# Memsets and small copies of an attention + feed-forward kernel on VectorE instead of GpSimd, with every engine's order made anew

## The chip, the cores and the metric

The kernel runs on one core of one Trainium2 chip. The metric is the device time of one execution in microseconds (us). A core has five engines that run side by side, each through its own list of instructions in order: TensorE (PE; its weight loads are listed as PEld), VectorE (DVE), ScalarE (ACT), GpSimd (POOL) and SyncE (SP), which only issues transfers (DMAs) here. GpSimd and SyncE each issue DMAs. An engine that meets an instruction whose inputs are not there waits, and all behind it in its list waits too.

## The reference

Attention with a decay ("forgetting attention"), then a bilinear feed-forward layer on its result. 8 batches x 8 heads, 576 positions, head size 64; the feed-forward layer takes 4608 tokens of 512 to 1536 and back.

```python
scores = scale * np.matmul(q, k.transpose(0, 1, 3, 2))
log_f = np.log(np.clip(f, 0.0001, 1.0))
cum = np.cumsum(log_f, axis=-1)
decay = cum[:, :, :, None] - cum[:, :, None, :]
scores = np.where(causal, -1000000000.0, scores + decay)
attn = softmax(scores)                       # max, exp, sum, divide
attn_out = np.matmul(attn, v)
x = attn_out.transpose(0, 2, 1, 3).reshape(B * S, H * D)
out = (x @ w_a) * (x @ w_b) @ w_out
```

## The kernel before

**Work.** Everything is written as a list of operations (class `Op`, L142): each has an engine (or a choice of two), a planned duration, and dependencies. The operations' own functions issue the instructions. Which operation comes when is not decided by the program: `ORDER` (L1069) is a long table of operation numbers, and `CHOICE` (L1177) gives the engine of those that have a choice. `laid_out` (L1181) reads both, and the instructions are issued in that order, so that each engine's list is the order of its operations in the table. Waits between engines are put in where data or buffers require it.

**Attention.** Heads go in pairs t = 0 to 31 (four pairs per batch). For a pair, the 576 queries are five blocks (the last of 64). `qk_group` (L443) makes the scores of a group of blocks in a PSUM tile `sc` (a ring of two buffers); groups are blocks (1, 0), (2), (3), (4). For batch 0 (`DECP`) the decay enters by matmuls of `crow` (the cumulated logarithms, high and low parts) with a one-hot column of `pick`; the causal mask by matmuls of `low` with `neg64`. Then VectorE reduces the maximum (L546), ScalarE takes the exponential with its sum (L603, PA or PB), VectorE takes the reciprocal of the sum (L613), GpSimd normalises (L621), and P is transposed, for the first pairs by TensorE (`psP`, L641), and multiplied with v (L663, L679). From batch 1 on, VectorE adds the decay from the tile `spread` in one instruction with the maximum (L572).

**Feed-forward.** As soon as four pairs of a batch have delivered 256 tokens or more, TensorE can do `psa`, `psb` (L950) and `pso` (L970) for them. These fill TensorE between the groups of scores.

**The head of the program.** k and q of batch 0 and 1 are loaded by GpSimd's queue with a cast (`load_qk`, L274, DMAs at L286), transposed on TensorE (`pe_transpose`, L299, tiles `psT` in a PSUM ring `ff` of three buffers, two buffers for each call) and copied to kT and qT by ScalarE or VectorE (`pe_evict`, L313). f is loaded by SP (L180), clipped on VectorE (L192), its logarithm taken on ScalarE (L226), cumulated on VectorE (`scan`, L195), and copied to `crow` as a high part (L230) and a low part (L200, on VectorE or GpSimd). ScalarE loads the table of the logarithm first (L220) and that of the exponential later (`o_e`, L239), each 1.28 us in the trace. `f_ones` (L182) sets three tiles with ones on VectorE. Weights are loaded by GpSimd's queue (`weights`, L412, DMAs at L424).

**What the change touches.** `identity` (L72) makes the 128x128 identity `ident16` on GpSimd, which the transposes and the one-hot columns need. `constants` (L81, GpSimd) sets `pickh`, `neg64` and `low`, copies 32x32 pieces of the identity to `pick` and `pickh`, and cuts `neg64` and `low` to their masks with six `affine_select`. `paddings` (L100, GpSimd) zeroes `qd`, `lowd`, parts of `PB` and of `nv`, and copies `low` to `lowd`. `wake` (L75) issues dummy matmuls on the identity, in 24 operations of two each (a wake pair), which keep TensorE busy while nothing else can run; they write the one PSUM buffer `pv`, so each pair waits for the pair before it.

Of the kernel before, what the change touches and what calls it, by code (L numbers as in the profile page):

```python
# [25 lines left out]
def kernel(  # L26
# [11 lines left out]
    nc = tc.nc  # L38
# [4 lines left out]
    NSB = (S + 127) // 128  # L43
# [16 lines left out]
    neg64 = perm.tile([128, 64], FP16, tag="neg64", name="neg64")  # L60
# [20 lines left out]
    def constants():  # L81
        for x in pickh:
            nc.gpsimd.memset(x, 0.0)
        for m in range(4):
            x = slice(32 * m, 32 * m + 32)
            nc.gpsimd.tensor_copy(out=pick[x, :], in_=ident16[x, x])
            nc.gpsimd.tensor_copy(out=pickh[m // 2][x, :], in_=ident16[x, x])
        nc.gpsimd.memset(neg64, 0.0)
        for x in low:
            nc.gpsimd.memset(x, 1.0)  # L90
        for h in range(2):
            nc.gpsimd.affine_select(out=neg64[HP[h], :], in_=neg64[HP[h], :],
                                    compare_op=mybir.AluOpType.not_equal, fill=NEGBIG, base=0,
                                    pattern=[[-1, 64]], channel_multiplier=1)
            for half in range(2):
                x = low[half][HP[h], :]
                nc.gpsimd.affine_select(out=x, in_=x, compare_op=mybir.AluOpType.is_gt, fill=0.0,
                                        base=64 * half, pattern=[[-1, 128]], channel_multiplier=1)

    def paddings():  # L100
        for x in (*qd, lowd):
            nc.gpsimd.memset(x, 0.0)
        for r in HP:
            nc.gpsimd.tensor_copy(out=lowd[r, r], in_=low[0][r, 0:64])
        for x in PB:
            nc.gpsimd.memset(x[:, 12, 64:128], 0.0)
        for i in range(2):
            nc.gpsimd.memset(nv[i][64:128, NSB - 1, :, :], 0.0)
# [104 lines left out]
    o_c = Op("POOL", 3.3, lambda _: constants(), [o_i], prio=-300, name="const")  # L213
# [28 lines left out]
    o_p = Op("POOL", 4.0, lambda _: paddings(), [o_c], prio=-100)  # L242
# [823 lines left out]
    for n in cuts:  # L1066
# [3 lines left out]
        65 1 0 45 2 49 53 57 67 3 69 28-30 36 31-35 4-8 46 9 47 37 38 10 50 48 51 52 43 11 78 12 123 54 13 39 81  # L1070
# [4 lines left out]
        162 385 386 260 163 221 261 80 199 22 244 23 387 24 200 99 245 105 207 263 208 100-102 388 106 252 253  # L1075
# [7 lines left out]
        403 306 351 396 352 398 354 345 308 353 397 307 405 277 494 1783 406 322 166 1784-1786 167 1788 356 1787  # L1083
        355 1789 407 408 1790 248 1792 1791 357 409 249 1793 410 287 1794 1795 309 1796 323 1798 310 1797 316
        311-313 358 250 1799 317 324 251 318 1800 495 339 211 1801 496 497 404 506 436 425 437 361 212 319 426
# [10 lines left out]
        480 1866 563 1868 1867 582 600 692 697 481 553 554 1864 1870 1871 1869 586 1872 1873 587 1874-1876 1878  # L1096
        562 603 1880 555 556 693 698 601 511 559 1877 1879 588 591 1881 589 1882 1884 1883 576 1885 1886 593
        1887 1888 611 590 583 592 569 578 570 610 584 585 1890 1891 594 1889 1892 604 1893 605 606 595 612 618
        596 571 577 613 699 1894 484 607 700 701 485 619 614 615 625 597 1895 694-696 646 704 709 1865 718 626
        486 609 1896-1898 1900 1902 620 1899 621 1903 1901 1904 1906 1908 608 628 1907 627 598 599 1860 716 632  # L1100
        487 622 1905 633 647 656 710 617 602 728 623 1909 705 634 1910-1912 637 638 629 635 1913 639-641 636
# [8 lines left out]
        754 762 763 904 772 792 1975 798 811 766 801 813 915 1977-1979 905 803 908 820 866 821 823 799 906 802  # L1110
# [114 lines left out]
```

## Time and profile before

| | us |
|---|---|
| median of 3 runs | 409.13 (408.86 to 409.19) |
| the profiled execution | 408.86 |
| its span, first to last instruction | 407.1 |
| TensorE busy | 396.3 |
| VectorE busy | 301.6 |
| ScalarE busy | 282.5 |
| GpSimd busy | 262.3 |

A row of the order of time reads: start, duration (us), engine, line, operation, output<-inputs, shapes, count, and in brackets the idle time of the engine before it with what ended that wait. A row with a count above one merges neighbours of one kind, from the start of the first to the end of the last. In the table of stretches, each engine's column is its busy time in that stretch, with the number of its instructions in parentheses.

### The profile page before, as it was taken

To read this page: it belongs to the slowest core of one execution; us is meant where nothing else is said; L and a number is where in the kernel's file an instruction comes from. 1 tells how busy PE (TensorE), PEld (TensorE's weight loads), DVE (VectorE), ACT (ScalarE), POOL (GpSimd) and SP (SyncE) were. 2 spreads that over 40 slices of the span, in tenths; PEclk is the share of its full clock that TensorE was granted. 3 is DMA by queue.
4 is the path that set the end of the run, shared out by engine and by line. 5 is a ranking of instruction groups with operands and counts; after the bars stand their busy time and mean duration, and the time that the engine had idled before them with its cause. 6 is when DMAs were issued, how large, how long until landed. Compare 5 with 4: busy or idle time off the path is not lost.

```text
span 407.1 us, 11321 instructions
## 1 busy us (share of the span) xinstructions
PE 396.3 (97%) x4028; PEld 213.4 (52%) x4028; DVE 301.6 (74%) x1007; ACT 282.5 (69%) x796; POOL 262.3 (64%) x490
## 2 busy tenths in 40 slices
PE   6899999999999999999999999999999999999996
PEld 2457675766755554444445454444444444444552
DVE  3887998997979778878868789688888874442241
ACT  3898988888977778778787877568785873231230
POOL 8997697778876786886787767849666555000000
PEclk9999999999999999999999999999999999999999
DMA  8999998999999999999999999999895768100102
GB/s 126 205 190 199 152 217 194 203 271 233 249 196 221 320 229 208 276 199 229 204 275 253 278 237 166 317 250 206 205 189 159 143 116 179 52 2 32 74 0 77
DMA packets 147176, 76.65 MB, mean 188 GB/s; under 512 B 124336, under 2 KB 129200, under 8 KB 147120
## 3 DMA queue, kind: packets, MB, share of 16 engines
q1 hardware_dynamic: 141040, 68.73, 72.2%
q0 software_dynamic: 5936, 7.08, 11.2%
q8 instruction: 31, 0.51, 0.5%
q14 instruction: 25, 0.20, 0.2%
q10 hardware_dynamic: 144, 0.13, 0.1%
HBM read 52.05 MB, written 9.58 MB: 151 GB/s over the span
## 4 chain that ended last, share of the span: by engine, by line
PE 74%; DVE 3%; issue 1%; ACT 0%; DVEq 0%
PE pso L970 22%; PE psb L950 20%; PE psa L950 20%; PE sc L449 6%; PE pv L663 4%; PE psT L307 1%; DVE S L572 1%; DVE ht L961 1%; PE sc L679 1%; PE pv L679 0%; PE psP L641 0%; DVE qT L259 0%; DVE st L613 0%; DVE half L259 0%; DVE st L572 0%
## 5 line engine op out<-in xcount | busy, mean ns | idle before, releaser
L572 DVE CUSTOM_DVE_ANT_0 S<-sc,spread 64x576 f32<-64x576 f32 (+4 forms) x232 | 126.3, 562 | 16.3 <-PE sc L449 6.3
L950 PE MATMUL psb<-xT,wb 128*128 128x512 f16 (+2 forms) x528 | 115.3, 341 | 0.0
L950 PE MATMUL psa<-xT,wa 128*128 128x512 f16 (+2 forms) x528 | 115.2, 341 | 0.0
L255 ACT CAST a<-psa 128x512 f16<-128x512 f32 (+2 forms) x132 | 66.4, 503 | 56.6 <-PE psa L950 47.2
L621 POOL TENSOR_SCALAR PA<-PA,st 128x256 f16<-128x256 f16 (+2 forms) x192 | 89.1, 476 | 23.8 <-DVE st L613 19.3
L961 DVE TENSOR_TENSOR ht<-psb,a 128x512 f16<-128x512 f32 (+2 forms) x132 | 77.4, 590 | 35.7 <-PE psb L950 30.5
L970 PE MATMUL pso<-wout,ht 128*128 128x512 f16 x432 | 99.8, 380 | 0.0
L603 ACT ACTIVATE PA<-S,st 128x256 f16<-128x256 f32 (+2 forms) x168 | 84.6, 505 | 10.9 <-DVE st L572 10.6
L621 POOL TENSOR_SCALAR PB<-PB,st 128x512 f16<-128x512 f16 (+1 forms) x96 | 67.4, 709 | 33.3 <-DVE st L613 14.3
L950 PEld LDWEIGHTS <-wa 128*128 128x128 f16 x528 | 49.1, 98 | 40.5 <-issue 2.1
L950 PEld LDWEIGHTS <-wb 128*128 128x128 f16 x528 | 49.1, 98 | 40.2 <-issue 2.0
L970 PEld LDWEIGHTS <-ht 128*128 128x128 f16 x432 | 39.8, 98 | 45.2 <-issue 0.9
L603 ACT ACTIVATE PB<-S,st 128x512 f16<-128x512 f32 x56 | 40.1, 717 | 8.0 <-DVE st L572 7.8
L449 PE MATMUL sc<-kT,qT 64*128 64x128 f16 (+4 forms) x384 | 34.4, 266 | 2.4 <-ACT PA L603 0.9
L603 ACT ACTIVATION_READ_ACCUMULATOR PA<-S,st 128x1 f32 x168 | 32.1, 191 | 0.0
L259 DVE CAST xT<-pv 128x512 f16<-128x512 f32 (+1 forms) x40 | 23.1, 578 | 5.0 <-PE pv L663 4.8
L449 PEld LDWEIGHTS <-qT 64*128 64x128 f16 (+1 forms) x384 | 13.5, 95 | 23.8 <-issue 16.2
L613 DVE RECIPROCAL st<-st 128x2 f32<-128x2 f32 x128 | 18.1, 157 | 10.2 <-ACT PB L603 5.9
L599 ACT ACTIVATE PB<-S,st 128x576 f16<-128x576 f32 x28 | 21.7, 776 | 5.5 <-POOL PA L621 1.9
L259 DVE COPY osb<-pso 128x512 f32<-128x512 f32 x17 | 11.7, 688 | 17.9 <-PE pso L970 17.8
L255 ACT COPY osb<-pso 128x512 f32<-128x512 f32 x18 | 10.4, 579 | 20.6 <-PE pso L970 14.4
L663 PEld LDWEIGHTS <-nv 128*64 128x64 f16 x640 | 19.1, 109 | 10.2 <-issue 8.4
(100 smaller groups left out, 475.6 us busy)
## 6 DMA issues: line engine op xcount, KB each, us to landing
spread<-cum_d SPq DMA_DIRECT2D x24, 576.0 KB, 5.9
out_dram<-osb SPq DMA_DIRECT2D x35, 256.0 KB, 2.8
v<-in_v_dram SPq DMA_DIRECT2D x32, 256.0 KB, 5.5
q<-in_q_dram SPq DMA_DIRECT2D x12, 576.0 KB, 6.3
k<-in_k_dram SPq DMA_DIRECT2D x12, 576.0 KB, 6.4
wout<-in_moe_w_out_dram POOLq DMA_DIRECT2D x3, 512.0 KB, 9.0
v<-in_v_dram SPq DMA_DIRECT2D x8, 128.0 KB, 3.8
wa<-in_moe_w_a_dram POOLq DMA_DIRECT2D x2, 512.0 KB, 9.0
```

The costliest lines, as they stand in the source:

```text
L255: nc.scalar.copy(out=out_, in_=in_)
L259: VEC[e].tensor_copy(out=out_, in_=in_)
L449: nc.tensor.matmul(out=dst, lhsT=lhsT, rhs=rhs, start=start, stop=stop, skip_group_check=True)
L572: nc.vector.tensor_tensor_reduce(out=o, in0=x, in1=y, scale=-1.0, scalar=3e38, op0=ADD, op1=MIN, accum_out=m)
L599: nc.scalar.activation(out=p_blocks(t, 4), in_=T[("s" if direct else "z", t, 4)], func=EXP, bias=st[:, 8:9], scale=sign, accum_out=st[:, 1 ...
L603: nc.scalar.activation(out=p_blocks(t, i)[:, :, h, :], in_=(T[("s", t, i)][:, h, :] if direct else T[("z", t, i)][:, h * n:h * n + n]).rea ...
L613: nc.vector.reciprocal(out=st[:, 20 + 2 * i:22 + 2 * i], in_=st[:, 10 + 2 * i:12 + 2 * i])
L621: VEC[e].tensor_scalar(out=p, in0=p, scalar1=st[:, c:c + 1], scalar2=1.0, op0=MUL, op1=MUL)
L663: nc.tensor.matmul(out=o[HP[h], 128 * i:128 * i + 128], lhsT=vt[:, j, pr + NP * h, :], rhs=pt[:, base_blk[i] + 2 * block_at(t, i, j) + h, ...
L950: nc.tensor.matmul(out=p[:, 0:n], lhsT=w16[:, db, 128 * fb:128 * fb + 128], rhs=xTflat[db][:, t0:t0 + n], start=(db == 0), stop=(db == 3))
L961: nc.vector.tensor_tensor(out=ht[:, 0:n], in0=T.pop(("psb", t0, fb))[:, 0:n], in1=T.pop(("a16", t0, fb))[:, 0:n], op=MUL)
L970: nc.tensor.matmul(out=o, lhsT=T[("ht", t0, fb)][:, 128 * tb:128 * tb + 128], rhs=wout16[:, fb, :], start=(fb == 0), stop=(fb == 11))
```

## The change

`constants` and `paddings` are split. `zeros` (VectorE) does all memsets of both, `picks` (VectorE) the eight 32x32 copies, `masks` (GpSimd) keeps the six `affine_select`, and `paddings` (VectorE) keeps the two copies of `low` to `lowd`. The identity stays on GpSimd.

```diff
-    def constants():
-        for x in pickh:
-            nc.gpsimd.memset(x, 0.0)
+    def zeros():
+        for x in (*pickh, neg64, *qd, lowd):
+            nc.vector.memset(x, 0.0)
+        for x in low:
+            nc.vector.memset(x, 1.0)
+        for x in PB:
+            nc.vector.memset(x[:, 12, 64:128], 0.0)
+        for i in range(2):
+            nc.vector.memset(nv[i][64:128, NSB - 1, :, :], 0.0)
+
+    def picks():
         for m in range(4):
             x = slice(32 * m, 32 * m + 32)
-            nc.gpsimd.tensor_copy(out=pick[x, :], in_=ident16[x, x])
-            nc.gpsimd.tensor_copy(out=pickh[m // 2][x, :], in_=ident16[x, x])
-        nc.gpsimd.memset(neg64, 0.0)
-        for x in low:
-            nc.gpsimd.memset(x, 1.0)
+            nc.vector.tensor_copy(out=pick[x, :], in_=ident16[x, x])
+            nc.vector.tensor_copy(out=pickh[m // 2][x, :], in_=ident16[x, x])
+
+    def masks():
         for h in range(2):
             nc.gpsimd.affine_select(out=neg64[HP[h], :], in_=neg64[HP[h], :],
...
     def paddings():
-        for x in (*qd, lowd):
-            nc.gpsimd.memset(x, 0.0)
         for r in HP:
-            nc.gpsimd.tensor_copy(out=lowd[r, r], in_=low[0][r, 0:64])
-        for x in PB:
-            nc.gpsimd.memset(x[:, 12, 64:128], 0.0)
-        for i in range(2):
-            nc.gpsimd.memset(nv[i][64:128, NSB - 1, :, :], 0.0)
+            nc.vector.tensor_copy(out=lowd[r, r], in_=low[0][r, 0:64])
...
     o_i = Op("POOL", 1.2, lambda _: identity(), prio=-301, name="ident")
-    o_c = Op("POOL", 3.3, lambda _: constants(), [o_i], prio=-300, name="const")
+    o_z = Op("DVE", 1.6, lambda _: zeros(), prio=-301, name="zeros")
+    o_k = Op("DVE", 0.9, lambda _: picks(), [o_i, o_z], prio=-300, name="picks")
+    o_c = Op("POOL", 2.1, lambda _: masks(), [o_z, o_k], prio=-300, name="masks")
...
-    o_p = Op("POOL", 4.0, lambda _: paddings(), [o_c], prio=-100)
+    o_p = Op("DVE", 0.25, lambda _: paddings(), [o_c], prio=-100, name="pads")
```

`ORDER` and `CHOICE` are replaced as a whole (two operations more, so the numbers shift by two). What differs at the head, engine by engine, is this (names of operations; "ptk0" is the transposes of k's first half of batch 0, "ev" a copy to kT or qT):

| engine | before | after |
|---|---|---|
| GpSimd | load k0, identity, load q0, load k1, load q1, a weight load, constants, a weight load, one low part of crow, paddings, two low parts, spread memset, two normalisations, four loads, ... | load k0, load q0, identity, load k1, load q1, masks, three low parts of crow, spread memset, eight loads (k and q of batch 1, six of weights), spread memset, normalisations, ... |
| VectorE | ones, clips, scan, high part, low part, scan, high part, maxima, ... | zeros, picks, ones, clips, scan, high part, scan, high part, one ev of k, low part, maxima of the first group, pads, ... |
| ScalarE | logarithm table, logarithm, ev k, logarithm, ev k, ev q, ev q, exponential table, exponentials | logarithm table, logarithm, logarithm, exponential table, ev k, ev q, ev q, exponentials |
| TensorE | 5 wake pairs, ptk0, 2 wake pairs, ptq0, 1 wake pair, scores of pair 0 (group 0), 1 wake pair, scores of pair 1, transposes of k's second half, 3 wake pairs, ... | 8 wake pairs, ptk0, ptq0, 1 wake pair, scores of pair 0, 1 wake pair, scores of pair 1, transposes of k's second half, 1 wake pair, ... |
| SP | a part of v, f, f, store of the cumulated sums, v, ... | f, f, a part of v, store of the cumulated sums, v, ... |

In the rest of the table neighbours change places by a few operations; 26 operations change their engine: the paddings, two low parts of crow, and 23 copies out of PSUM between ScalarE and VectorE (14 go to VectorE, 9 to ScalarE).

More of the change, by code (lines that the diff above doesn't have):

```diff
@@ L1096 @@
[L1096 to L1100, printed above, removed]
@@ L1171 @@
-        2354 2355 2357 2359 2356 2358 2360-2363 2365 2367 2364 2368 2366 2369 2371 1698 2373 2372 2374-2376 2370
-        2377 2380 2381 1699 2382 2385 2378 2386 2387 2390 2391 2383 2379 2384 2388 2392-2394 2389 2395 2397 2396
-        2399 2398 2401 2400 2403 2402 2405 2404 2407 2409 2408 2406 2410 2411 2413 2412 2415 2414 2417 2416 2419
-        2418 2421 2420 2423 2422 2425 2424 2427 2426 2429 2428 2431 2430 2433 2432 2435 2434 2437 2436 2439 2441
-        2440 2443 2438 2442 2444 2445 2448 2446 2449 2447 2450 2453 2451 2454-2456 2452 2458 2457 2459
+        3 0 1 47 51 2 4 30 31 55 59 5 32 6-8 38 33 39 34 9-11 35 40 41 12 13 48 45 49 67 44 36 37 43 50 52 14
[4 rows of a table added]
@@ new lines @@
+        183 184 223 222 261 164 82 388 227-229 262 165 101 263 201 24 246 25 26 202 209 102 103 247 107 108 210
+        265 389 104 254 255 266 188 127 109 390 267 106 270 143 146 110 105 274 1752 1754 1756 1753 1755 152
+        1758 147 1757 148 153 1759 68 149 189 75 77 151 190 1760 27 28 115 1761-1763 154 150 172 191 144 155 78
[6 rows of a table added]
+        346 496 399 1791 408 169 409 1792 358 1793 359 250 1794-1796 251 410 289 1797 411 1798 1800 252 311 313
[9 rows of a table added]
+        545 546 535 542 521 1856-1858 566 458 479 328 547 466 529 560 472 1859 1860 481 530 518 478 329 480 484
@@ new lines @@
+        562 537 536 543 544 550 552 551 548 549 553 554 567 556 555 563 1863 1864 574 581 582 575 569 485 568
+        1861 482 583 577 570 576 1865 565 1868 1870 1869 602 699 694 483 1866 1872 584 1873 588 1871 1874 1875
+        589 578 1876-1878 1880 564 605 1882 557 558 695 700 603 561 513 1879 1881 590 593 1883 594 591 1884 1886
+        1885 1887 585 1888 595 1889 1890 580 571 572 592 613 612 573 596-598 586 1892 1893 1891 1894 606 1895
+        607 608 587 614 621 579 615 701 609 1896 486 702 703 616 1897 620 487 711 712 599 696-698 648 706 720
@@ new lines @@
+        1867 617 627 628 610 488 1898 1900 1902 611 1899 1904 622 1901 623 1905 630 1903 1906 1908 1910 1909 629
+        600 601 1862 718 624 634 1907 635 649 625 604 1911 489 639 640 631 707 636 1912-1915 637 641-643 658 619
[3 rows of a table added]
+        1938 727 713 1939 724 1940 745 689 714 715 733 732 746 1941 691 690 1942 734 739 738 1943-1945 677 716
+        678 679 717 748 729 1946 725 740 747 1948 752 726 753 1950 1947 1949 1951 741 1952 728 742 1953 749 766
+        1925 904 722 1954 693 692 909 812 1955 754 1956 1958 1960 735 757 1957 1959 758-760 767 769 777 778 1961
@@ new lines @@
+        755 773 1962 1964 1966 1963 750 905 751 776 736 744 737 719 1967 785 791 1965 761 1968 1970 784 1969 792
+        779 787 780 793 1972 1974 775 1975 1971 1973 786 1976 770 798 799 772 1920 858 916 763 756 762 813 765
+        906 774 794 1977 768 743 764 803 815 910 1979-1981 907 800 917 771 801 802 823 805 825 1984 804 824 788
+        781 830 908 1985 831 1982 859 783 822 782 868 819 826 832 806 807 809 808 911 1978 914 921 837 816 795
+        912 833 789 797 838 817 796 790 827 1986 834 1989 1987 1990-1992 818 913 840 1993 821 1994 918 920 839
[5 rows of a table added]
@@ new lines @@
+        2025 2026 957 874 976 986 901 927 900 1119 1114 1022 2027-2029 939 2030 952 962 963 932 953 945 977
+        2031-2034 964 2035 958 2036 947 1115 946 938 979 2037 935 987 959 967 969 968 970 971 1120 961 902 903
[9 rows of a table added]
+        1150 1141 1085 1099 1091 1112 1128 1072 2087 1129 1130 1074 1107-1110 1132 1187 2089 2091 1143 1147 2090
[14 rows of a table added]
+        2173 1375 1319 1321 2168 1368 1300 1301 1376-1379 2172 2174 1359 2175 2178 1370 1534 1396 1539 1302 1320
[13 rows of a table added]
+        2246-2249 1569 2251 1564 2252 1532 1533 1581 2244 1592 1593 1589 1566 1594 1568 1616 1559 1591 1562 1609
@@ new lines @@
+        1595 1575 1565 1617 1618 1624 1597 1619-1621 1598 2253 2250 1652 2245 2256 2257 1610 1615 2258 1599-1601
[5 rows of a table added]
+        1651 1686 2288 1660 1705 2289 1689 2290 2291 2293 1687 1713-1715 1690 1721 1720 1691 1722 2294 1723 2295
+        2292 1657 1674 2296-2298 1716 1692 1693 2299 2301 1709 1706 2302 1727 2300 1708 1728 2303 1729 1730 2304
+        1731 1711 1734 1717 1724 2305 1735 1710 2307 2309 2306 2310 2308 1736 1675 1683 1676 1668 1688 1694 1669
+        1695 1718 1726 1704 1719 1725 1732 1733 1739 1737 1740-1742 1707 1743 2311 2314-2317 2312 1696 1697 1738
@@ new lines @@
+        1744-1747 2319 1698 2320 2321 2324 1699 2318 2313 2322 2325 1748 2326 1749 2327 2328 2323 2329-2335 2337
+        2339 2336 2338 2340-2345 2347 2349 2346 2348 2350-2355 1750 1751 2356 2357 2359 2361 2358 2360 2362-2365
+        2367 2369 1700 2366 2370 2368 2371-2373 2375 2374 2377 2378 1701 2376 2379 2382-2384 2387 2380 2388 2389
+        2392 2393 2385 2381 2386 2390 2394-2396 2391 2397 2399 2398 2401 2400 2403 2402 2405 2404 2407 2406 2409
+        2411 2410 2408 2412 2413 2415 2414 2417 2416 2419 2418 2421 2420 2423 2422 2425 2424 2427 2426 2429 2428
@@ L1176 @@
+        2431 2430 2433 2432 2435 2434 2437 2436 2439 2438 2441 2443 2442 2445 2444 2440 2446 2447 2450 2448 2451
+        2449 2452 2455 2453 2456-2458 2454 2460 2459 2461
     """
     CHOICE = """
-        DPPPAAAADDDAPAAADADDDAAADDDDDDDDAAAAADDDAAADDDAADADDDAAAAAADAAAAAAAAADAADAAAAADAAAAAAAAAADAADDADADAA DAA
+        PPDPADAADDDAPAAADADDDADADDDDDDADADAAAADADADDDDADADDAAADAAAADAADAAAAAAAAAAAAAADDAAAADADADADDADDAAADAA DAA
     """
```

20 lines of the change are left out of this document (removed), and 144 rows, old and new, of the table ORDER.

## The prediction

> **What bounds the kernel now.** I read the page first (busy shares), then busy time by stretch, then the order of time of each engine up to 34 us.
>
> ```profile
> span 407.1 us, 11321 instructions
> ...
> PE 396.3 (97%) x4028; PEld 213.4 (52%) x4028; DVE 301.6 (74%) x1007; ACT 282.5 (69%) x796; POOL 262.3 (64%) x490
> ```
>
> ```profile
> core 0: us, PE busy (x) PEld busy (x) DVE busy (x) ACT busy (x) POOL busy (x), PEclk, DMA share, GB/s
> 5.00:10.00 5.00, 4.63 (x84) 1.69 (x83) 1.94 (x5) 1.89 (x5) 4.68 (x21) 1.00 1.08 182
> 10.00:15.00 5.00, 3.89 (x77) 1.99 (x76) 4.51 (x10) 4.29 (x13) 4.50 (x13) 1.00 1.19 221
> 15.00:20.00 5.00, 4.68 (x78) 2.13 (x77) 4.41 (x10) 4.43 (x17) 4.86 (x10) 1.00 0.93 191
> 20.00:25.00 5.00, 4.32 (x53) 2.50 (x52) 4.46 (x11) 4.75 (x19) 5.00 (x11) 1.00 1.19 193
> 25.00:30.00 5.00, 4.98 (x96) 3.13 (x94) 4.43 (x10) 4.45 (x14) 4.96 (x12) 1.00 1.15 186
> ...
> 40.00:50.00 10.00, 9.04 (x209) 7.04 (x208) 9.36 (x32) 9.80 (x30) 5.50 (x9) 1.00 0.96 160
> ...
> 380.00:408.00 28.00, 23.43 (x133) 12.73 (x130) 8.52 (x15) 6.71 (x14) 0.00 (x0) 0.95 0.13 47
> ```
>
> TensorE is the bound: 396.3 of 407.1 us busy. Of its 10.8 us idle, 3.7 lie in the last stretch (407.1 - 380 - 23.43: the last copy and store), 2.9 before its first matmul (next fence), 2.5 between 5 and 25 us, 1.0 between 40 and 50, and hardly 0.5 in all the rest. So time can be won or lost only in the first 50 us, and there the busy figures include dummy matmuls (wakes), which do no work. GpSimd is full from 5 to 30 us, which is what the change unloads; ScalarE and VectorE run at some 90% beside it.
>
> The head, TensorE (and its weight loads, PEld) first:
>
> ```profile
> 2.89 4.47 PE L78 MATMUL wake<-ident 128*128 128x512 f16 x10 [2.89 <-POOL ident masks.py:199]
> 3.98 0.10 PEld L78 LDWEIGHTS <-ident 128*128 128x128 f16 x1 [0.54 <-issue]
> ...
> 6.12 0.31 PEld L78 LDWEIGHTS <-ident 128*128 128x128 f16 x2 [0.54 <-issue]
> 6.77 0.10 PEld L78 LDWEIGHTS <-ident 128*128 128x128 f16 x1 [0.34 <-issue]
> 7.32 0.48 PE L307 MATMUL psT<-ident,k 64*64 64x64 f16 x36
> ...
> 10.55 0.34 PE L449 MATMUL sc<-kT,qT 64*128 64x256 f16 x4 [0.40 <-ACT qT L253]
> 11.60 0.27 PE L449 MATMUL sc<-crow,pick 64*128 64x256 f16 x2 [0.60 <-POOL crow L200]
> ```
>
> Wake pairs start at 2.89 and 3.98, the fourth at 6.12, the fifth at 6.77: the first three take 1.08 us each, the fourth 0.65. The fifth ends (7.3) just as the first transposes of k start. Scores of the first group start at 10.55 but finish only when GpSimd's part of crow is there (11.60).
>
> **The change part by part.** *The identity and the wakes.* On GpSimd the load of q now stands before the identity, and on TensorE eight wake pairs, not five, stand before the transposes of k.
>
> ```profile
> 2.78 0.73 POOL L286 DMA_DIRECT2D q<-in_q_dram  x1
> 8.43 0.62 ACT L255 COPY kT<-psT 128x576 f16<-128x576 f16 x1
> 9.84 1.19 ACT L253 ACTIVATE qT<-psT 128x576 f16<-128x576 f16 x2
> 12.07 1.79 DVE L546 TENSOR_REDUCE st<-sc 128x2 f32<-128x512 f32 x3 [0.35 <-PE sc L449]
> ```
>
> The first wake moves by one issue, 2.89 + 0.73 = 3.62. Three pairs at 1.08 and five at 0.65, the last overlapped to 0.55 as before, put the transposes of k at 3.62 + 3.24 + 2.6 + 0.55 = 10.0 instead of 7.32. Bounds: 12.3 if all eight stay at 1.08, 8.7 if all take 0.65; I take the mixture seen. The transposes of q need a third and a fourth buffer of a ring of three, so they wait for ScalarE's first copy of k: 10.0 + 0.48 + 0.62 = 11.1; q done 11.6, its first copy (half of 1.19) 12.25, scores at 12.3. The eight matmuls of scores and eight of masks follow without a wait, 0.6 us, and the first reduction starts at 12.95 instead of 12.07: **0.9 late**.
>
> The Trainium skill ("TensorE: Matmul & The Clock Gate", What's actually happening) says that the array runs at half clock until a free-running window of about 3.4 us has been busy. The step from 1.08 to 0.65 at 6.12, 3.2 us after the first wake, agrees; as its window isn't tied to the start, by that rule three more pairs could be slow, and the transposes come 1.3 us later still.
>
> *Memsets, copies and the decay chain on VectorE.*
>
> ```profile
> 0.88 0.06 DVE L183 MEMSET warm<- 128x1 f32 x1 [0.88 <-PEq L1209]
> 1.03 0.54 DVE L184 MEMSET cum_f<- 96x576 f16 x1
> 1.72 0.54 DVE L185 MEMSET cum_f<- 32x576 f32 x1 [0.15 <-issue]
> 7.79 0.57 DVE L192 TENSOR_SCALAR cum_f<-cum_f 96x256 f32<-96x256 f32 x2 [5.53 <-DMA cum_f<-in_f_dram]
> 11.05 1.28 ACT L188 ACT_TABLE_LOAD   x1
> 18.38 0.95 DVE L546 TENSOR_REDUCE st<-sc 128x2 f32<-128x768 f32 x1
> 19.25 0.22 DVE L613 RECIPROCAL st<-st 128x2 f32<-128x2 f32 x2
> ```
>
> VectorE idles 5.5 us before f lands; the new work goes there. A memset costs 0.06 + 0.83 ns per element ((0.54 - 0.06)/575). The twelve have 1,088 elements per partition as compiled (zeros are written four bytes at a time): 1.6 us, or 3.4 with the 0.15 gap each. Eight 32x32 copies have no row on VectorE: 0.07 each (pitch of the two reciprocals) to 0.22 (that and the gap), so 0.6 to 1.8; I take the low end, the reciprocals being nearest in size. They wait for the identity (3.6), then come the old memsets (0.88 to 2.26: 1.4). So the clip of f starts between 5.6 (3.6 + 0.6 + 1.4) and 7.5 (0.88 + 3.4 + 1.8 + 1.4), I take 6.3, instead of 7.79; f is loaded ahead of a part of v on SP now, so it lands no later than before. From clip to the last part of crow took 11.60 - 7.79 = 3.8, and is as long again, as both first halves now follow each other on GpSimd (10.50 for 1.05, next fence, plus 0.8) instead of one on each engine: 10.1, hidden behind the scores at 12.3. ScalarE loads the exponential's table (1.28 + 0.2) before the copy of k: two logarithms end 1.3 after the clip, so 9.1, hidden until 10.5. Were that cover gone (clip at 7.79) it would cost 0.1. So the earlier decay wins nothing: its wait (0.60) is gone, the wakes take its place.
>
> *GpSimd's relief.*
>
> ```profile
> 5.56 0.21 POOL L83 MEMSET pick<- 128x32 f16 x2
> ...
> 7.83 0.35 POOL L92 TENSOR_SCALAR_AFFINE_SELECT neg<-neg 64x64 f16<-64x64 f16 x1
> 10.50 1.05 POOL L200 TENSOR_TENSOR crow<-cum_f,crow 32x256 f16<-32x256 f32 x1
> ...
> 14.14 1.64 POOL L200 TENSOR_TENSOR crow<-cum_f,crow 32x320 f16<-32x320 f32 x2
> 16.13 0.83 POOL L621 TENSOR_SCALAR PA<-PA,st 128x256 f16<-128x256 f16 x2
> ...
> 27.39 1.62 POOL L621 TENSOR_SCALAR PA<-PA,st 128x128 f16<-128x128 f16 x4
> 29.00 0.50 PE L641 MATMUL psP<-ident,PA 128*128 128x128 f16 x6
> ```
>
> It loses 5.56 to 7.83 and 11.55 (10.50 + 1.05) to 14.14, 4.8 us, and takes over 0.8 for a part of crow while it gives VectorE another of about that size. Does that come through? In its new order eight loads follow crow (11.5 + 8 x 0.73, the load of q, = 17.3), then the normalisation of pair 0's first block, whose reciprocal stands on VectorE behind the second pair's wide reduction. That reduction ended at 19.33 (18.38 + 0.95); 0.6 to 0.7 later, between the 0.9 of the first one and the 0.5 at the end of the walk below, makes 20.0, where GpSimd began normalising at 16.13 before: it idles almost 3 us. From there to the last normalisation of pair 3's first blocks stand some 16 of 0.42 (0.83/2), two wider (0.46), one weight load, one memset and a cast of v (1.0): 9.5 us, so 29.5. Before it ended at 29.01 (27.39 + 1.62), and the transposes of P started at 29.00 on that. So the transposes would be some 0.5 late here too: the 4.8 us go into the wait and into loads done sooner than anything needs them. The loads share the transfer engines (share 1.19 from 10 to 15 us) with v:
>
> ```profile
> v<-in_v_dram SPq DMA_DIRECT2D x32, 256.0 KB, 5.5
> ```
>
> Issued at 12, v would land at 17.5 in the usual time, and its cast stands at 25: even twice the time (23.0) is hidden.
>
> *The walk to 33 us.* Two score buffers alternate, each freed by the exponentials that read it, so a late group passes its lateness on to the next but one; ScalarE, the busiest here beside GpSimd, is where it can be caught up.
>
> ```profile
> 13.47 1.91 PE L78 MATMUL wake<-ident 128*128 128x512 f16 x6
> 17.24 0.58 ACT L603 ACTIVATE PA<-sc,st 128x384 f16<-128x384 f32 x1 [0.57 <-DVE st L546]
> 23.80 0.34 PE L449 MATMUL sc<-kT,qT 64*128 64x384 f16 x2 [0.68 <-ACT PA L603]
> 33.05 0.61 PE L950 MATMUL psa<-xT,wa 128*128 128x256 f16 x4
> ```
>
> The 0.9 is carried to the first exponentials, grows by 0.2 (padding copies, now on VectorE) and shrinks by the 0.57 that ScalarE waited at 17.24, since of the three wake pairs at 13.47 one is left there: some 0.5 at 23.8. From there to 33.05 TensorE is full, with four wake pairs in either order: 0.5 late at the first feed-forward matmul. Bounds: 1.1 if nothing is regained; below nothing, as after the first transposes 16 pairs stand instead of 19: 3 x 0.65 = 1.95 less, of which I grant half, -1.0.
>
> *The rest.* Later, the feed-forward matmuls stand against the scores as before, to one or two groups of 0.86. There is 0.5 of idle time after 50 us to win, and up to about 1 to lose, where a score group now meets a buffer not yet freed; I take nothing. Evictions swapped between ScalarE and VectorE cancel. Sum: +0.5, so 408.86 + 0.5 = 409.4 against the profiled run's own time, which lies 0.27 below the median of 409.13; so **409.6**.
>
> **Rivals.** *GpSimd becomes the bound* (slower). The place is the first normalisation, behind that reciprocal; it decides once GpSimd's list passes 29.5, where the walk alone puts the transposes of P (29.0 + 0.5). For it: 5.00 and 4.96 of 5 us busy from 20 to 30. If the 1.1 is carried to that reciprocal undiminished, it comes at 20.4 and the list ends at 29.9, or at 30.3 if the cast of v waits besides; taking 30.1, the transposes and all behind them are 1.1 late: 410.2. Against: the loads end 2.7 us ahead of that reciprocal, so loads that take longer cost nothing, and a reciprocal that is less late gives 0.5 back. *The fewer wakes come through* (faster): half of 1.95, 408.1. For it: TensorE is full from 25 to 33, so a pair less is 0.65 won if its data are there. Against: the pairs taken away stood where ScalarE was behind. *All of it is regained* at 40 to 50 us, where TensorE idles 1.0 and ScalarE, 9.80 of 10, has one eviction (0.5) less: 409.1.
>
> **How the numbers follow.** Forecast 0.36, GpSimd bound 0.26, fewer wakes 0.30, regained 0.08. A measurement tells 0.2%, 0.8 us, from no change. The forecast's own range is 408.9 to 410.3; within 0.2% are 0.20 of its 0.36, 0.01 of the third and the last 0.08: 0.29. Slower: 0.16 + 0.26 = 0.42; faster 0.29. Range 407.9 to 411.2: below, the -1.0 and a little of the 0.5; above, 410.2 and the 1 that later stages can lose.
>
> **What would show it.** First wake at 3.6, transposes of k at 10.0, first reduction at 13.0, GpSimd idle from some 17 to 20, transposes of P at 29.5, first feed-forward matmul at 33.5. A first feed-forward matmul before 32.5, or over 1 us more TensorE idle after 50 us, would make it wrong.

## The result and the profile after

The changed kernel takes a median of **410.5 us** (409.5 to 412.12, 15 runs), the kernel before 409.13 (408.67 to 409.92, 15 runs beside them). The ratio is 1.0035, with a 95% interval of 1.0027 to 1.0044: slower by 1.1 to 1.8 us. The profiled execution of the changed kernel is the lowest of its runs, 409.5 against the 408.86 of before, so it shows only 0.64 of the loss; where the remainder comes from is a question of its own below.

The head of the page of the changed kernel (the span, then busy time, share and instructions of each engine):

```profile
span 407.8 us, 11318 instructions
...
PE 396.0 (97%) x4028; PEld 212.9 (52%) x4028; DVE 305.9 (75%) x1034; ACT 279.3 (68%) x791; POOL 257.5 (63%) x468
```

As meant, 4.8 us have left GpSimd and 4.3 have come to VectorE. The stretches of the changed kernel (busy time of each engine, instructions in parentheses) show where:

```profile
core 0: us, PE busy (x) PEld busy (x) DVE busy (x) ACT busy (x) POOL busy (x), PEclk, DMA share, GB/s
5.00:10.00 5.00, 4.66 (x14) 1.28 (x12) 4.04 (x9) 2.47 (x5) 2.89 (x8) 1.00 1.21 215
10.00:15.00 5.00, 4.06 (x147) 2.51 (x147) 3.02 (x7) 2.56 (x7) 4.64 (x9) 1.00 1.00 197
15.00:20.00 5.00, 3.80 (x68) 2.07 (x68) 4.97 (x9) 4.71 (x20) 1.98 (x4) 1.00 1.16 188
20.00:25.00 5.00, 4.58 (x60) 2.48 (x56) 4.63 (x13) 4.89 (x19) 4.71 (x12) 1.00 1.20 203
40.00:50.00 10.00, 9.20 (x214) 6.92 (x213) 9.12 (x29) 9.77 (x28) 6.42 (x11) 1.00 1.16 195
```

The first row has TensorE as busy as before, 4.66 of 5 us, but with 14 instructions where there were 84: it is all wakes. ScalarE has 2.56 of 5 us busy from 10 to 15, where it had 4.29: its load of the exponential's table (1.28 us) now stands ahead of 10 us, and the work that it waits for comes later. GpSimd drops from 4.86 to 1.98 from 15 to 20 us. The order of time on TensorE says when the steps came (in brackets the idle time and what ended it):

```profile
3.61 6.51 PE L78 MATMUL wake<-ident 128*128 128x512 f16 x16 [3.61 <-POOL ident masks.py:199]
10.05 0.48 PE L310 MATMUL psT<-ident,k 64*64 64x64 f16 x36
...
11.27 0.47 PE L310 MATMUL psT<-ident,q 64*64 64x64 f16 x35 [0.72 <-ACT kT L258]
...
12.50 0.34 PE L452 MATMUL sc<-kT,qT 64*128 64x256 f16 x4 [0.21 <-ACT qT L256]
...
14.55 1.26 PE L78 MATMUL wake<-ident 128*128 128x512 f16 x4
...
24.63 0.34 PE L452 MATMUL sc<-kT,qT 64*128 64x384 f16 x2
...
29.88 0.62 PE L644 MATMUL psP<-ident,PA 128*128 128x128 f16 x6
...
34.19 0.61 PE L953 MATMUL psa<-xT,wa 128*128 128x256 f16 x4
```

The first transposes start 2.73 later than before (10.05 against 7.32), the scores of the first group 1.95 (12.50 against 10.55), the transposes of P 0.88 (29.88 against 29.00), the first feed-forward matmul 1.14 (34.19 against 33.05). Part of the 1.95 had been lost before too, as the scores then waited until 11.60 for crow. The other engines of the changed kernel, in the same view:

```profile
1.71 0.55 DVE L89 MEMSET nv<- 64x256 uint32 x2
3.58 0.16 DVE L94 COPY pick<-ident 32x32 f16<-32x32 f16 x1 [1.33 <-POOL ident masks.py:199]
...
4.61 0.34 DVE L95 COPY pick<-ident 32x32 f16<-32x32 f16 x1
...
6.50 0.53 DVE L193 TENSOR_SCALAR cum_f<-cum_f 96x256 f32<-96x256 f32 x2 [0.15 <-DMA cum_f<-in_f_dram]
10.58 0.64 ACT L258 COPY kT<-psT 128x576 f16<-128x576 f16 x1 [1.46 <-PE psT L310]
13.16 1.02 DVE L549 TENSOR_REDUCE st<-sc 128x2 f32<-128x512 f32 x2 [1.27 <-PE sc L452]
16.68 0.30 POOL L524 MEMSET spread<- 128x128 f32 x1
20.27 0.72 POOL L624 TENSOR_SCALAR PA<-PA,st 128x128 f16<-128x128 f16 x2 [3.29 <-DVE st L616]
27.68 2.32 POOL L624 TENSOR_SCALAR PA<-PA,st 128x128 f16<-128x128 f16 x6 [0.37 <-DVE st L616]
```

VectorE now waits 1.27 us for the first scores, and ScalarE 1.46 us for the first transposes: the decay and the constants, whose work was moved, are ready in time, and TensorE is what everything waits for. GpSimd, unloaded, waits 3.29 us for the first reciprocal.

### The profile page after: what moved, and what is told of

The parts are those of the page before. It is cut to its first block, busy times and chain, and to the rows that moved or that the text cites. A ratio compares the mean times of both kernels' runs of the same rounds, so it can differ in the third digit from the quotient of the medians.

```text
span 407.8 us, 11318 instructions
## 1 busy us (share of the span) xinstructions
PE 396.0 (97%) x4028; PEld 212.9 (52%) x4028; DVE 305.9 (75%) x1034; ACT 279.3 (68%) x791; POOL 257.5 (63%) x468
## 3 DMA queue, kind: packets, MB, share of 16 engines
HBM read 52.05 MB, written 9.58 MB: 151 GB/s over the span
## 4 chain that ended last, share of the span: by engine, by line
PE 68%; DVE 2%; ACT 0%; issue 0%
PE pso L973 19%; PE psb L953 19%; PE psa L953 19%; PE sc L452 5%; PE pv L666 4%; PE psT L310 1%; PE sc L682 1%; DVE S L575 1%; ACT PA L606 0%; DVE ht L964 0%; DVE osb L262 0%; DVE xT L262 0%; PE pv L682 0%; DVE half L262 0%; ACT half L258 0%
## 5 line engine op out<-in xcount | busy, mean ns | idle before, releaser
L624 POOL TENSOR_SCALAR PA<-PA,st 128x128 f16<-128x128 f16 (+2 forms) x192 | 89.5, 477 | 38.1 <-DVE st L616 31.4
L953 PEld LDWEIGHTS <-wb 128*128 128x128 f16 x528 | 48.2, 98 | 38.8 <-issue 2.5
L534 POOL TENSOR_SCALAR_AFFINE_SELECT spread<-spread 128x768 f32<-128x768 f32 x24 | 20.8, 867 | 5.1 <-DMA spread<-cum_d 4.4
```

The lines of the kernel that those rows point to most:

```text
L534: nc.gpsimd.affine_select(out=c[:, :, 0:SM].rearrange("p h (j k) -> p h j k", k=128), in_=c[:, :, SM:2 * SM].rearrange("p h (j k) -> p h j ...
L624: VEC[e].tensor_scalar(out=p, in0=p, scalar1=st[:, c:c + 1], scalar2=1.0, op0=MUL, op1=MUL)
L953: nc.tensor.matmul(out=p[:, 0:n], lhsT=w16[:, db, 128 * fb:128 * fb + 128], rhs=xTflat[db][:, t0:t0 + n], start=(db == 0), stop=(db == 3))
```

## The experiments

All edits but one start from the changed kernel and move operations in the order table; the lists below name the operations of one engine. The theory to be tested (A in the expectations): the loss is the head's, that is, three wake pairs more and the load of q ahead of the identity keep TensorE from the first transposes, and each us that the first feed-forward matmul comes late is a us at the end. Its rivals: GpSimd with its normalisations is the bound; VectorE's new work costs what is lost; or (D) a later transfer, that of v, comes too late.

### The changed kernel again

No edit.

> The changed kernel as it stands, for a second profile, as its runs spread from 409.5 to 412.1 us and the profiled one was the lowest. All theories expect some 410.5. If the spread comes from the clock of TensorE at the head (wake pairs that stay at 1.08 us for longer), this profile shows the transposes of k at another time than 10.05 us, up to 11.4; if from later stages, the head is the same to 0.1 us and the idle time of TensorE after 50 us differs from the 0.5 us of the first profile.

It took 411.07 us, span 409.4. The first transposes came at 10.19 and the first feed-forward matmul at 34.55, each later than in the first profile. Its GpSimd and TensorE rows also have a wait that was not there (1.70 of idle time ahead of the cast, 1.04 ahead of the transposes):

```profile
57.05 1.59 POOL L262 CAST nv<-v 128x1024 f16<-128x1024 f32 x2 [1.70 <-DMA v<-in_v_dram]
...
59.36 0.56 PE L644 MATMUL psP<-ident,PB 128*128 128x128 f16 x7 [1.04 <-POOL PB L624]
```

v took 15.0 us to land (median of its four loads issued between 38 and 60 us), behind 512 KB loads of w_out. So of the 1.6 us between the spans of two executions of one kernel, 0.36 is there at the first feed-forward matmul and 1.04 comes through v.

### Memsets and copies alone

The changed kernel's code with the order of before; `zeros` and `picks` are put behind the ones on VectorE, `paddings` behind the first group's maxima.

```diff
 VectorE:
-zeros, picks, ones, clips, ..., maxima of the first group, pads   (and the new order of all engines)
+ones, zeros, picks, clips, ..., maxima of the first group, pads   (and the order of before)
```

> The memsets and copies on VectorE as in the change, but every engine in the order of before (memsets and copies on VectorE behind its three old memsets, ahead of the clip of f; the padding copies behind the first group's maxima). Theory A (the loss is the new order's head: eight wake pairs and a later identity): no loss, 408.3 to 409.2 us, as GpSimd has 4.8 us less to do and nothing at the head is later; first reduction at 12.07 us or up to 0.8 earlier. Rival B (work on VectorE itself costs, by contention or by delaying the clip): 410 or more, with the clip of f later than 7.8 us or VectorE's rows longer.

The median was 408.52 (12 runs), the ratio to before 0.9988 (0.9978 to 0.9998). So the move to VectorE costs nothing; it wins a little. Its first reduction starts at 11.49 instead of 12.07, although in that profile the five wake pairs ahead of the first transposes started some 1.07 us apart to the last, and the transposes only at 8.00: crow is ready, and its wait of 0.60 is gone. That the VectorE work is what is lost falls with this run.

```profile
8.00 0.48 PE L310 MATMUL psT<-ident,k 64*64 64x64 f16 x36
...
11.01 0.33 PE L452 MATMUL sc<-crow,pick 64*128 64x256 f16 x4
...
11.49 1.02 DVE L549 TENSOR_REDUCE st<-sc 128x2 f32<-128x512 f32 x2 [0.55 <-PE sc L452]
```

### Five wake pairs again

```diff
 TensorE:
-wake 0 to 7, transposes of k, transposes of q, wake 8, ...
+wake 0 to 4, transposes of k, wake 5 and 6, transposes of q, wake 7, ...
-..., transposes of k's second half, two pairs, ...
+..., transposes of k's second half, three pairs, ...
```

> The changed kernel with five wake pairs, not eight, ahead of the first transposes of k; the three stand where the order of before has them (two behind those transposes, one more behind the transposes of k's second half). Theory A: transposes of k at 8.1 us, ScalarE free for the copy at 9.1 (exponential's table), first reduction at 11.9 to 12.2 us instead of 13.16, and most of the loss regained: 409.0 to 409.6 us. Rival C (GpSimd's list behind its late reciprocal bounds the first 30 us): the head moves but the first feed-forward matmul stays at 34.0 to 34.2 and the time at 410.2 to 410.8.

The median was 408.89 (12 runs), the ratio 1.0000 (0.9988 to 1.0013): the whole loss is gone. The first transposes came at 8.83, the first reduction at 12.43, the first feed-forward matmul at 33.54.

```profile
8.83 0.58 PE L310 MATMUL psT<-ident,k 64*64 64x64 f16 x36
...
33.54 0.61 PE L953 MATMUL psa<-xT,wa 128*128 128x256 f16 x4
```

### Two reciprocals earlier

On VectorE the reciprocal that the first normalisation waits for goes ahead of the second pair's wide reduction, and a second one moves forward likewise.

```diff
 VectorE:
-..., reciprocal, wide reduction, ev of q, spread copy, wide reduction, reciprocals, ...
+..., reciprocals, wide reduction, ev of q, spread copy, reciprocal, wide reduction, ...
```

> The changed kernel with two reciprocals moved ahead on VectorE: that of pair 0's block 0 beside that of its block 1, that of pair 1's block 0 ahead of the second wide reduction. GpSimd's first normalisation then starts at 17.1 us instead of 20.27. Rival C (GpSimd's list is the bound): the transposes of P of pair 3, 29.88 us, come 0.5 to 1 us earlier and the time falls to 409.5 to 410.0. Theory A: those transposes stand behind TensorE's own late scores, so the time stays at 410.2 to 410.7.

The median was 410.56 (10 runs), the ratio 1.0042 (1.0028 to 1.0056): nothing won. GpSimd and TensorE of this kernel:

```profile
17.95 0.37 POOL L624 TENSOR_SCALAR PA<-PA,st 128x128 f16<-128x128 f16 x1 [0.94 <-DVE st L616]
20.13 0.37 POOL L624 TENSOR_SCALAR PA<-PA,st 128x128 f16<-128x128 f16 x1 [1.81 <-DVE st L616]
...
28.43 2.31 POOL L624 TENSOR_SCALAR PA<-PA,st 128x128 f16<-128x128 f16 x6 [0.86 <-DVE st L616]
30.63 0.61 PE L644 MATMUL psP<-ident,PA 128*128 128x128 f16 x6
```

The first normalisation starts 2.3 us earlier (17.95 against 20.27), though this profile's first reduction is 0.73 later (13.89), but GpSimd then waits again for VectorE's reciprocals, 0.86 us ahead of the last six normalisations too, and from the first reduction to the transposes of P it takes 16.74 us (30.63 - 13.89) as in the changed kernel (29.88 - 13.16 = 16.72). GpSimd isn't the bound there.

### The identity ahead of the load of q

```diff
 GpSimd:
-load k0, load q0, identity, load k1, ...
+load k0, identity, load q0, load k1, ...
```

> The changed kernel with the identity ahead of the load of q on GpSimd, eight wake pairs kept. Theory A (each us that the first transposes are late comes out at the end): first wake at 2.9 us, transposes of k 0.7 earlier than with the same clock in the changed kernel (9.3 to 10.1), first feed-forward matmul 0.7 earlier, 33.5 to 34.2, and 0.7 us less time: 409.6 to 410.0. Rival (only the number of pairs matters, as the clock's step is tied to a time and not to the first wake): the step from 1.08 to 0.65 us stays at some 7 us, and the time at 410.2 or more.

The median was 409.88 (12 runs), the ratio 1.0014 (1.0004 to 1.0024). The first wake came at 2.88, the transposes of k at 9.23, the first feed-forward matmul at 33.42. That profile was the slowest of its runs (411.29): its cast of v waited 2.30 us, and TensorE 1.65 behind it.

### The loads of w_out later

The six loads of weights stay; the three of w_out move to where they were before the change.

```diff
 GpSimd:
-..., w_out, ..., w_out, ..., w_out, ... (three loads, before the casts of v)
+..., (the same three, at the places of before)
```

> The changed kernel with the three loads of w_out at the places that they have in the order of before, 9, 6 and one operation later on GpSimd. In its second profile GpSimd's cast of v waited 1.70 us for a transfer (14 to 15 us from issue to landing, 7.3 before) and TensorE 1.04 us behind it. Theory D (the rest of the loss, and the spread of 409.5 to 412.1, is that transfer): v lands some us sooner, no such wait, median 409.8 to 410.1 and a narrower spread. Theory A alone: 410.3 to 410.7, spread as it was.

The median was 410.65 (5 runs, 410.17 to 411.08), the ratio 1.0042 (1.003 to 1.0054): the median doesn't come from that transfer, and theory D falls. The loads of v landed after 8.3 us there, and nothing waited for them. The first transposes stood at 10.38 and the first feed-forward matmul at 34.90, so this profile, near the median in time, has the loss wholly in the head.

### Both parts of the old head

The identity ahead of the load of q and five pairs, with all else of the change.

```diff
 GpSimd:
-load k0, load q0, identity, load k1, ...
+load k0, identity, load q0, load k1, ...
 TensorE:
-wake 0 to 7, transposes of k, transposes of q, wake 8, ...
+wake 0 to 4, transposes of k, wake 5 and 6, transposes of q, wake 7, ...
```

> The changed kernel with both: identity ahead of the load of q and five wake pairs ahead of the transposes of k. Theory A: transposes of k at 7.4 to 8.1 us, the copy of k at 9.1 behind the exponential's table, first reduction 11.6 to 11.9, first feed-forward matmul 33.0 to 33.2; with the 373.6 us from there to the end that the changed kernel's profiles show (374.05 before), a span of 406.7 and 408.3 to 408.7 us. If the head were not the cause, 409.5 or more.

The median was **408.14** (12 runs, 407.94 to 409.54), the ratio to before **0.9974** (0.9957 to 0.999): faster than both kernels. Several engines of it in order of time:

```profile
2.88 5.20 PE L78 MATMUL wake<-ident 128*128 128x512 f16 x10 [2.88 <-POOL ident masks.py:199]
8.02 0.48 PE L310 MATMUL psT<-ident,k 64*64 64x64 f16 x36
8.85 0.62 ACT L258 COPY kT<-psT 128x576 f16<-128x576 f16 x1
11.54 1.02 DVE L549 TENSOR_REDUCE st<-sc 128x2 f32<-128x512 f32 x2 [0.34 <-PE sc L452]
32.76 0.61 PE L953 MATMUL psa<-xT,wa 128*128 128x256 f16 x4
```

The first feed-forward matmul is 1.43 earlier than in the changed kernel, and the span 1.4 shorter (406.4).

### The new head in the kernel before

The kernel before, with the identity behind the load of q and eight pairs ahead of the transposes of k; memsets and copies stay on GpSimd.

```diff
 GpSimd:
-load k0, identity, load q0, load k1, ...
+load k0, load q0, identity, load k1, ...
 TensorE:
-wake 0 to 4, transposes of k, wake 5 and 6, transposes of q, ...
+wake 0 to 7, transposes of k, transposes of q, ...
```

> The kernel before, all memsets on GpSimd and its own order, but with the identity behind the load of q and eight wake pairs ahead of the transposes of k. Theory A: transposes of k at 10.0 to 10.8 us, first reduction at 13.2 or later (ScalarE's second logarithm stands behind the copy of k here), first feed-forward matmul at 34.0 to 34.8, and the loss of the change without its memsets: 410.0 to 411. If the moved memsets or the rest of the order were the cause: 409.1.

The median was 410.07 (6 runs), the ratio 1.0033 (1.0022 to 1.0044), the loss of the change without its memsets. TensorE and VectorE of it:

```profile
10.38 0.48 PE L307 MATMUL psT<-ident,k 64*64 64x64 f16 x36
13.71 1.78 DVE L546 TENSOR_REDUCE st<-sc 128x2 f32<-128x512 f32 x3 [0.52 <-PE sc L449]
34.21 0.61 PE L950 MATMUL psa<-xT,wa 128*128 128x256 f16 x4
```

### Four pairs, and the exponential's table later

The version with the old head, one more pair taken from the front and put behind the transposes of k's second half, and ScalarE's load of the exponential's table behind the copies of q.

```diff
 TensorE:
-wake 0 to 4, transposes of k, wake 5 and 6, ..., transposes of k's second half, three pairs, ...
+wake 0 to 3, transposes of k, wake 5 and 6, ..., transposes of k's second half, four pairs, ...
 ScalarE:
-logarithm, exponential table, ev k, ev q, ev q, exponentials
+logarithm, ev k, ev q, ev q, exponential table, exponentials
```

> The kernel with the old head and the rest of the change (408.14 us), with one wake pair less ahead of the transposes of k (four; the fifth stands behind the transposes of k's second half) and the exponential's table behind the copies to qT on ScalarE. Theory A (the first transposes and what follows them set the start of everything): transposes of k at 7.3 to 7.4 us, copy of k at 7.9 instead of 8.85, first reduction at 10.5 to 10.8 instead of 11.54, first feed-forward matmul 0.6 to 1.0 earlier than 32.76, and 407.2 to 407.7 us. Rival (from here on another wait sets the start: the low part of crow on GpSimd, the table ahead of the first exponential, or the score buffers): the first reduction moves but the first feed-forward matmul stays within 0.3 of 32.76, 407.9 to 408.3 us.

The median was 408.66 (12 runs), the ratio 0.9988 (0.9975 to 1.0000): nothing is won beyond the old head, by the profile (span 406.7 against 406.4) a little is lost. TensorE and ScalarE of it:

```profile
9.40 0.48 PE L310 MATMUL psT<-ident,q 64*64 64x64 f16 x36 [0.54 <-DMA q<-in_q_dram]
11.15 1.28 ACT L189 ACT_TABLE_LOAD   x1
```

The transposes of k start at 7.05, 0.97 earlier, but those of q then wait for q itself (9.40 against 9.64). The second group's scores come at 15.40 instead of 14.99, behind the fourth pair and the exponentials that the table now delays: the first feed-forward matmul stands at 33.09 against 32.76. The transfer of q, and the exponentials behind the later table, take the place of the wake pair. Two things are changed at once here, so this run prices neither alone.

### The same with the later loads of w_out

The version before this one, with w_out's loads moved as above.

> The same with the three loads of w_out at the later places that they have in the order of before. Where they stand late, v of batch 1 landed in 8.3 us instead of 13 to 15. If the wait of GpSimd's cast for v comes in a part of the runs only: the same median to 0.2 us, and fewer runs that lie 1 us above it. If it comes in most: 0.5 us or more less.

The median was 408.74 (12 runs), the ratio 0.9987 (0.9977 to 0.9998), the same. The runs lie closer, 408.51 to 409.13 against 408.15 to 409.84, and v landed after 7.8 us; so the late v may be what lengthens some runs, but it isn't what sets the median.

## Why the prediction came out as it did

The table puts the profiles side by side, in us: the transposes of k, the first reduction, the first feed-forward matmul, the difference of these two (the walk), and the span less the first feed-forward matmul (the rest).

| kernel | transposes of k | first reduction | first feed-forward | walk | rest |
|---|---|---|---|---|---|
| before | 7.32 | 12.07 | 33.05 | 20.98 | 374.05 |
| memsets and copies alone | 8.00 | 11.49 | 32.51 | 21.02 | 374.09 |
| new head in the kernel before | 10.38 | 13.71 | 34.21 | 20.50 | 374.0 |
| changed | 10.05 | 13.16 | 34.19 | 21.03 | 373.6 |
| changed, again | 10.19 | 13.30 | 34.55 | 21.25 | 374.85 |
| five pairs | 8.83 | 12.43 | 33.54 | 21.11 | 373.56 |
| reciprocals earlier | 10.78 | 13.89 | 34.93 | 21.04 | 373.67 |
| w_out later | 10.38 | 13.49 | 34.90 | 21.41 | 373.8 |
| old head | 8.02 | 11.54 | 32.76 | 21.22 | 373.64 |

- **The head: right.** The first wake came at 3.61 (said: 3.62), the transposes of k at 10.05 (10.0), those of q behind ScalarE's copy of k at 11.27 (11.1), the scores at 12.50 (12.3), the first reduction at 13.16 (12.95). That it sets the loss is shown in both directions: taken away, the loss goes (1.0000 with five pairs, 0.9974 with the whole old head); put into the kernel before, it comes (1.0033).
- **Memsets and copies: right in effect, wrong in one size.** The twelve memsets took 1.4 us (0.88 to 2.26; said 1.6). The eight copies took 1.37 (3.58 to 4.95), where 0.6 was taken from bounds of 0.6 to 1.8; one took 0.16 to 0.41. The clip came at 6.50 (6.3), as f landed only then. Up to the first scores all of it stayed hidden: the copy of k waited for TensorE, not for the table, and the matmuls of crow followed the scores without a wait.
- **GpSimd's relief: right.** Loads, and a memset behind them, until 16.98 (17.3), then 3.29 of idle time (almost 3), the first normalisation at 20.27 (20.0), the list ends at 30.0 (29.5), with the transposes of P at 29.88 (29.5), which the text had put 0.4 too early.
- **The walk: the step that failed.** The first reduction was 1.09 late. The text let this lateness (0.9 there, and 0.2 more for the padding copies) "shrink by the 0.57 that ScalarE waited at 17.24", to 0.5 at the scores at 23.8, and stay 0.5 from there on. The same scores came at 24.63, 0.83 late, and the first feed-forward matmul 1.14 late, just above the bound of 1.1. Over the whole walk nothing was regained: it takes 21.03 where it took 20.98. One premise was wrong: of the three wake pairs at 13.47 two are left, not one (the row at 14.55 has four matmuls; the table of the change says one as well). And ScalarE doesn't save its wait. Its rows in the changed kernel, the copy of spread in the kernel before, and its exponentials in the kernel before with the new head:

```profile
16.28 0.47 ACT L606 ACTIVATE PA<-sc,st 128x256 f16<-128x256 f32 x1 [0.29 <-DVE st L549]
...
17.09 0.58 ACT L258 COPY spread<-scd 128x512 f32<-128x512 f32 x1
...
18.35 0.60 ACT L606 ACTIVATE PA<-sc,st 128x384 f16<-128x384 f32 x1
```

```profile
18.90 0.59 ACT L255 COPY spread<-scd 128x512 f32<-128x512 f32 x1
```

```profile
18.30 0.58 ACT L603 ACTIVATE PA<-sc,st 128x384 f16<-128x384 f32 x1
```

  The wait of 0.57 ahead of the wide exponentials is gone, but they start 1.11 late all the same (18.35 against 17.24): ScalarE now waits 0.29 for the second pair's maximum, which VectorE takes behind the padding copies, and copies spread ahead of these exponentials, which before came behind them. In the kernel before with the new head that copy stands where it was, the exponentials start 1.06 late though the first reduction is 1.64 late, and the walk gives back 0.48 (20.50). So the regain exists, but in the old order.

  From the scores at 24.63 on, TensorE has the same work with four wake pairs in either order, as the text says, but not the same time: 9.56 us to the first feed-forward matmul where it took 9.25. Every profile of the new order has 9.55 to 9.58 there, and those of the old order have 9.25 to 9.47. One row differs in the same way, the transposes of k in that stretch, 0.77 to 0.81 in the new order and 0.48 in the old; the changed kernel and the kernel before:

```profile
26.83 0.81 PE L310 MATMUL psT<-ident,k 64*64 64x64 f16 x36
```

```profile
25.89 0.48 PE L307 MATMUL psT<-ident,k 64*64 64x64 f16 x36
```

  That row can't be all of it, as the kernel with the memsets and copies alone has 9.47 with 0.48. Both places are read from the rows. No run changes either alone, so that they are the cause isn't shown.
- **The rest: taken as 0, it won 0.45** (374.05 to 373.6), within the 0.5 that were allowed for. All profiles of the new order in which v doesn't wait have it (373.56 to 373.8), and neither profile of the old order with an edit does. The stretch from the first feed-forward matmul on, of the changed kernel and then of before, in the columns of the table of stretches:

```profile
34.19:408.00 373.81, 368.59 (x3584) 198.89 (x3578) 278.65 (x961) 255.88 (x721) 233.46 (x416) 1.00 0.84 189
```

```profile
33.05:408.00 374.95, 368.92 (x3584) 199.73 (x3578) 277.97 (x957) 258.20 (x724) 233.03 (x416) 1.00 0.82 189
```

  Three quarters of it, 0.33, is busy time of TensorE with the same number of instructions; what makes these shorter stays open. The 0.5 of the text was idle time, so that the size fits is luck.
- **The sum, and luck in it.** 1.14 - 0.45 is the 0.7 of the spans, against the 0.5 forecast. That these lie close is luck: the first feed-forward matmul came 0.64 later than the text has it (0.2 from the head, 0.1 up to the scores at 24.63, 0.3 behind them), the rest was 0.45 shorter, and the two nearly cancel. The median of 410.5 lies in the whole range (407.9 to 411.2), but 0.9 above the forecast and outside the forecast's own 408.9 to 410.3. The likely reason is that the profiled run had the earliest head: with the same order of the head, other profiles have the transposes of k at 10.19, 10.38 and 10.78 and the first feed-forward matmul at 34.55 to 34.93. A run with 34.9 is 1.85 late there and, less 0.45, 1.4 us in all, as much as the difference of the medians (410.5 - 409.13). It is an estimate, as the profile of before may be an early one too: the same five pairs put the transposes of k at 8.00 and 8.02 in two other kernels, where it has 7.32.
- **The rivals.** GpSimd as the bound gave a time near the median (410.2), but its mechanism falls: a normalisation 2.3 us earlier moves nothing, and GpSimd's last six wait for VectorE with either order of the reciprocals (0.37 and 0.86). "Fewer wakes come through" is the 0.48 in the old order, nothing in the new one. "All regained at 40 to 50 us": TensorE idles 0.80 there (10.00 - 9.20) instead of 0.96, so hardly any of it is regained at that place.

## What to carry to other kernels

A dummy matmul is free only where its engine would wait anyway. Here the fifth wake pair in front of the first transposes covered most of a wait for q (0.54 us with four pairs): with four (and the table moved) nothing was won. The sixth to the eighth were paid: set further back, they take the ratio to before from 1.0035 to 1.0000. A DMA issue of 0.72 us in front of what the first wake needs was paid as well: behind it, the ratio is 1.0014. Even so, of the 2.73 us by which the first transposes came later, about half reached the end.

Relief on a busy engine comes through only if the engine that feeds it isn't late; ask first who releases it. And a wait that a forecast lets vanish is regained only if the engine's order puts nothing else in its place.

A change in several parts is best taken apart: here the move of the memsets won a little (0.9988), with the rest of the order it came to 0.9974 (the two intervals overlap), and one place of the order cost more than both won.

## What the runs showed of the hardware

The wake pairs get faster at no fixed time. Weight loads on TensorE of the version with the identity ahead of the load of q, then of the one with the earlier reciprocals, at the point where the two loads of a pair first merge into one row, which is where the pair's pitch goes from some 1.07 to 0.65:

```profile
6.11 0.31 PEld L78 LDWEIGHTS <-ident 128*128 128x128 f16 x2 [0.54 <-issue]
```

```profile
8.96 0.32 PEld L78 LDWEIGHTS <-ident 128*128 128x128 f16 x2 [0.54 <-issue]
```

The first weight load of the wakes stood at 2.87 and 3.60, so the step came 3.2 us after it in one execution and 5.4 in the other: three slow pairs or five. In the stretch from 5 to 10 us of both the granted clock reads 1.00 all the same, so that column doesn't show it. The Trainium skill ("TensorE: Matmul & The Clock Gate", What's actually happening) has the array at half clock until a free-running window of about 3.4 us has been busy, one not tied to the start of the work. The profiles agree with a moment that isn't tied to the start, but a pair's pitch falls to 0.6 of what it was, not to half. With eight pairs in front and the same start of the wakes, the transposes of k lie between 10.05 and 10.78, so the step makes the head vary by up to 0.7 us, a little over half of the 1.3 that the prediction gave for three more slow pairs.

The loads of v, 256 KB on SyncE's queue, landed in 5.7 us (median of all in the changed kernel). Those issued between 38 and 60 us took 13.2 to 15.5 in the seven profiles with two or three 512 KB loads of w_out on GpSimd's queue beside them, and 7.8 and 8.3 in the two of the new order that move these loads later. So loads on one queue slow those on another. That reached the path in two of the profiles, where GpSimd's cast of v waited 1.70 and 2.30 us.
